# First batch's local attention heads: 32-row query blocks with VectorE's transpositions, or 64-row blocks with TensorE's

## The chip, the cores and the metric

The kernel runs on one core of a Trainium2 chip. Its time is that of the whole program on the device, in microseconds. Three runs of the kernel before took 515.04, 516.04 and 516.3 us, with a median of 516.04 us. TensorE (PE) multiplies matrices, VectorE (DVE) and ScalarE (ACT) do element-wise work, GpSimd (POOL) and SyncE (SP) issue DMA transfers.

## The reference, cut to what matters

Three parts follow each other for a batch of 4, 576 tokens and 8 heads of 64: sparse attention, a channel-mixing block, and four small attention experts. Only the first part is touched. Its first four heads are "local": a query sees itself and the 31 keys before it.

```python
scores = scale * np.matmul(q, k.transpose(0, 1, 3, 2))
mask_local = (rel >= 0) & (rel < stride)                      # stride 32
mask_strided = (rel >= 0) & (pos[None, :] % stride == pos[:, None] % stride)
masks = np.stack([mask_local if h < H // 2 else mask_strided for h in range(H)], axis=0)
scores = np.where(masks[None, :, :, :], scores, -1000000000.0)
scores = scores - np.max(scores, axis=-1, keepdims=True)
attn = np.exp(scores)
attn = attn / (np.sum(attn, axis=-1, keepdims=True) + 1e-09)
x = np.matmul(attn, v)                                        # then the heads side by side
xk = mu_k * x + (1.0 - mu_k) * x_prev ; xr = mu_r * x + (1.0 - mu_r) * x_prev
v = np.maximum(xk @ w_k, 0.0) ** 2 @ w_v ; r = sigmoid(xr @ w_r) ; x = r * v
# x goes on to four gated attention experts, 576 causal tokens each
```

## The kernel before, in words

Nothing is issued where it is written. A recorder (class `Recorder`, lines 185 to 484) collects each operation; `unit` (line 240) names groups of them, and the string `PLAN` (line 21) lists the names in an order of preference. `order` (line 382) is a list scheduler: with costs of its own for each operation it gives each engine's queue, always the operation that it expects to start first, and within 0.1 us of that the one whose unit stands first in `PLAN`. A load into a tile that is still in use isn't given before the scheduler has placed the tile's last user. Where the scheduler expects TensorE to wait within its first 80 us, `warm` (line 371) puts products on a tile of zeros ahead of the waiting operation; they write the result tile that this operation then overwrites, and so bear its name in the trace (`sl<-zeros`). Every engine runs its queue in order.

A name in `PLAN` begins with the batch (0 to 3). `L` with a pair of heads loads its queries, keys and values; of batch 0 it is split into `q`, `v` and `m`, and a plain `0L0` to `0L19` there loads a piece of a weight, `0W` makes it a whole float32, and `0P` splits it into a high and a low part. `S` is scores and softmax, `T` the transposition, `V` the product with the values. `A` and `Z` with r, k, g, m, v are the mixing block's two token chunks (rows 0 to 319 and 320 to 575): preparing its inputs, gates, the first and the second product. Names without a batch's stage letter after `mc` belong to the experts.

Heads go in pairs. Pairs 0 and 1 are local, 2 and 3 strided (`strided_group`, line 844). A local pair is done by `local_part` (line 785) in two parts, `S0` and `S1` for pair 0, `S3` and `S4` for pair 1. The 128 partitions of a score tile hold 2 heads x 2 halves of the sequence (rows 0 to 287 and 288 to 575) x a block of 32 queries, and its columns 5 or 4 such blocks with 64 keys each. `softmax_exp` (line 661) does for each block a masked maximum on VectorE (`CUSTOM_DVE_ANT_0`, tile `el`) and an exponential on ScalarE; `softmax_norm` (line 681) divides on VectorE. VectorE then transposes the 32x32 blocks (`STREAM_TRANSPOSE`, tile `aTl`), and 40 small value products per pair (`pol`) add up in PSUM over both parts, with one unit `V1` or `V4` for the pair. `evac` (line 553) copies a result from PSUM on ScalarE or VectorE, as the scheduler picks.

Loads are in `load`, `load_rest` and `load_more` (lines 710 to 783). Of batch 0's local pairs `near` brings queries and keys in four transfers for blocks 0 to 4 of both halves and four for the rest; `keys` brings the values in eight, which GpSimd issues for batch 0 and SP for the others. The local mask arrives as `mraw`, and six copies on VectorE make the 32-row mask `mloc` of it. Batch 0's local pairs and later those of batch 1 use the two buffers of tile `qkv`.

The first token chunk's gates of batch 0 (`pr<-xw`, units `0Ag0` to `0Ag2`) are the first long products on TensorE; the first of them needs heads 0 to 3 of batch 0 and two pieces of the weight `w_r`.

Of the kernel before, what the change touches and what calls it, by code (L numbers as in the profile page):

```python
# [27 lines left out]
0P8 1Ar0 2L3 0Zm4 2S0 1V8 1Ak0 2S1 1T9 1Ar1 1Ar2 0Zm5 1Ak2 1Zr0 1V9 1Ak1 0Zm6 1Ar3 1Ak3 0Zm7 2S4 2S3 1Zr2 1Zk0 0Zv6  # L28
0Zv2 0P2 0Av7 0P3 0Zv7 1Am0 1Zr3 0Zv4 0Zv0 1Zr1 2V1 1Zk2 2V4 2S7 2Ar0 1Zk1 2S6 1Ag1 3z 1Am1 1Ag3 1Ag0 2T7 1Ag2 0Zv3
1Am2 1Am3 0Zv5 2Zr0 1Am4 2T6 1Zg2 1Am5 2S8 0Zv1 1Zk3 3L1 2V6 2S9 1Zg1 1Am6 2V7 3L0 1Zg0 2T8 1Zg3 2Ar2 1Av0 1Am7 1Av4  # L30
2T9 1Av6 1Zm0 1Zm1 1Zm2 2V9 2V8 1Av2 2Ak0 1Zm3 2Ar3 1Zm4 1Zm5 1Av5 1Zv0 1Av3 1Zm6 1Zm7 1Zv1 1Zv6 2Ak3 1Zv2 2Ar1 2Ak1
2Ak2 1Av1 2Zr2 1Zv4 1Zv7 3L2 3S4 1Av7 2Am0 2Zk0 2Zr3 2Am1 3L3 2Am2 2Ag1 2Ag0 2Ag3 2Am3 1Zv5 2Zr1 3S1 3S0 2Ag2 3S3
3S7 2Av0 3S6 2Am4 3S9 1Zv3 3V1 2Am5 2Am6 2Zg1 2Zk3 2Am7 3S8 3V4 2Zg2 2Zk2 2Zg0 3T7 2Av4 2Zk1 3T6 2Zg3 3V7 2Zm0 2Av6
2Av7 3V6 3T8 2Zm1 2Zm2 3T9 2Zm3 2Av5 3V9 2Av2 2Av3 2Av1 2Zm4 2Zm5 2Zm6 2Zv2 2Zm7 2Zv0 3V8 2Zv6 2Zv4 3Ar0 2Zv1 2Zv7
2Zv3 2Zv5 3Ar1 3Ar2 3Ar3 3Ak0 3Ak1 3Ak2 3Ak3 3Ag0 3Ag1 3Ag2 3Ag3 3Zr0 3Zr1 3Zr2 3Zr3 3Am0 3Am1 3Am2 3Am3 3Am4 3Am5
3Am6 3Am7 3Zk0 3Zk1 3Zk2 3Zk3 3Zg0 3Zg1 3Zg2 3Zg3 wl0 ws00 3Av0 3Av1 3Av2 ws01 3Av3 3Av4 3Av5 wl1 ws10 3Av6 3Av7
ws11 3Zm0 3Zm1 3Zm2 wl2 ws20 3Zm3 3Zm4 3Zm5 3Zm6 ws21 3Zm7 3Zv0 3Zv1 wl3 ws30 3Zv2 3Zv3 3Zv4 ws31 3Zv5 3Zv6 3Zv7 mc
0u 0x0 0k00 0q00 0k01 0q01 0v0 0v1 0x1 0k10 0q10 0k11 0q11 0t 0v2 0v3 0v4 0g 1u 1n 1x0 1k00 0s20 0s21 0s22 1q00 0s23
0s30 1k01 0s31 0s32 1q01 0s33 0m2 0p20 0p21 1v0 0p22 0p23 0s40 1v1 0s41 1x1 1k10 0s10 0m3 1q10 1k11 0s11 0p31 0p33
1q11 0s00 1s20 0m4 0p32 0s13 0s02 0s03 0s01 0p41 0p40 0p30 2x0 2k00 1s23 0s12 2x1 1v2 1s21 1v3 1s30 0m0 1s00 1g 2q01  # L40
0a10 0a11 1s33 1s31 0m1 2k10 1t 2q10 0p11 1s22 0p00 1s03 1s32 2s30 0p13 0o13 0p10 1s01 1m3 0p03 0o11 1m2 2v4 0p01
# [1517 lines left out]
```

## Time and profile before

| | before |
|---|---|
| median of 3 runs | 516.04 us (515.04 to 516.3) |
| profiled execution, its own time | 518.32 us |
| span of that execution | 516.5 us |
| busy: PE, DVE, ACT, POOL | 508.1, 366.5, 301.5, 46.6 us |
| share of the span | 98%, 71%, 58%, 9% |
| chain that ended last | PE 92%, DMA 3%, DVE 3%, ACT 1%, issue 1% |
| granted TensorE clock, mean | 0.997 |

Busy time is an average over stages with different limits: the share of an engine says little until it is read stage by stage. All instructions come from the recorder's line 482, so rows are told apart by their tiles: `sl`, `el`, `aTl`, `pol` are local scores, probabilities, transposed probabilities and results; `ss`, `es`, `pts`, `aTs`, `pos` the same for strided heads; `pr` gates; `xT` the attention's output. A float32 matmul is two MATMUL instructions, a transposition one.

### The profile page before, as it was taken

Reading aid. Unit: us, or ns where it says so; the run is one execution under the profiler, and the core shown is the slowest. Engines: PE = TensorE matmul, PEld = TensorE weight load, DVE = VectorE, ACT = ScalarE, POOL = GpSimd, SP = SyncE. Lnnn points to the kernel's source line nnn. Section 1 sums busy time; section 2 is a strip of 40 time slices with the busy share of each in tenths; the row PEclk is TensorE's granted clock in tenths of the full one; section 3 lists DMA queues with packets and bytes.
Section 4 is the critical chain, followed back from the end, with each engine's and each line's share of the span. In section 5 each row is a group of like instructions: output and inputs, shape, how many; then the busy total and the mean of one; then the engine's idle time right before and its main releaser. Section 6 shows DMA issues by size and latency. Waiting matters only on the chain.

```text
span 516.5 us, 12855 instructions
## 1 busy us (share of the span) xinstructions
PE 508.1 (98%) x4938; PEld 478.1 (93%) x4938; DVE 366.5 (71%) x1320; ACT 301.5 (58%) x893; POOL 46.6 (9%) x104
## 2 busy tenths in 40 slices
...
GB/s 227 330 222 413 129 26 46 136 73 184 10 84 14 90 34 22 11 83 89 67 31 94 82 77 27 31 145 127 70 98 72 51 64 102 32 81 47 13 103 93
...
## 3 DMA queue, kind: packets, MB, share of 16 engines
...
q8 instruction: 39, 0.64, 0.6%
q14 instruction: 22, 0.18, 0.1%
...
## 4 chain that ended last, share of the span: by engine, by line
PE 92%; DMA 3%; DVE 3%; ACT 1%; issue 1%; SPq 0%; ACTq 0%; DVEq 0%
PE pv L482 20%; PE pk L482 20%; PE pr L482 11%; PE pq_True L482 5%; PE pvv L482 5%; PE s L482 5%; PE pq_False L482 5%; PE pt L482 4%; PE pw L482 4%; PE py L482 3%; PE sl L482 3%; PE ss L482 3%; PE pol L482 3%; PE pos L482 2%; PE pts L482 1%; DVE pe L482 1%
## 5 line engine op out<-in xcount | busy, mean ns | idle before, releaser
L482 PE MATMUL pv<-kk,wvh 128*128 128x320 f32 (+1 forms) x512 | 102.8, 295 | 0.0
L482 PEld LDWEIGHTS pv<-kk,wvh 128*128 128x128 f32 x512 | 81.6, 188 | 0.5 <-DVE nm L482 0.2
L482 PE MATMUL pk<-xh,wkh 128*128 128x256 f32 (+1 forms) x224 | 66.6, 297 | 0.0
L482 PE MATMUL pk<-xl,wkh 128*128 128x256 f32 (+1 forms) x224 | 65.3, 291 | 0.0
L482 ACT ACTIVATE rf<-pk 128x320 f32<-128x320 f32 (+1 forms) x64 | 26.1, 407 | 48.9 <-PE pk L482 47.7
L482 ACT ACTIVATE pe<-pe,nm 128x128 f32<-128x128 f32 (+4 forms) x72 | 41.9, 582 | 15.9 <-DVE nm L482 8.0
L482 DVE CAST kk<-rf 128x256 fp32r<-128x256 f32 (+1 forms) x43 | 13.2, 307 | 43.1 <-ACT rf L482 26.9
L482 PEld LDWEIGHTS pk<-xh,wkh 128*128 128x128 f32 x224 | 42.0, 188 | 0.6 <-ACT rf L482 0.2
L482 PEld LDWEIGHTS pk<-xl,wkh 128*128 128x128 f32 x224 | 42.0, 188 | 0.0
L482 DVE CUSTOM_DVE_ANT_0 pe<-s,mcau 128x384 f32<-128x384 f32 (+4 forms) x72 | 33.5, 481 | 5.0 <-PE s L482 4.0
L482 ACT ACTIVATE es<-es,nm 108x108 f32<-108x108 f32 (+1 forms) x80 | 30.2, 381 | 6.6 <-DVE nm L482 6.6
L482 DVE TENSOR_TENSOR sg<-pv,sg 128x320 f32<-128x320 f32 (+1 forms) x32 | 14.5, 452 | 26.0 <-PE pv L482 19.8
L482 PE MATMUL pt<-ident,pe 128*128 128x128 f32 x200 | 30.6, 274 | 0.1
L482 DVE TENSOR_TENSOR kk<-rf,kk 128x320 fp32r<-128x320 f32 (+1 forms) x64 | 28.7, 455 | 2.4 <-ACT kk L482 1.2
L482 ACT ACTIVATE el<-el,nm 128x64 f32<-128x64 f32 x72 | 24.2, 337 | 9.0 <-DVE nm L482 8.8
L482 ACT ACTIVATE rf<-rf 128x320 f32<-128x320 f32 (+1 forms) x64 | 28.4, 444 | 1.3
L482 PE MATMUL pr<-xh,wrh 128*128 128x320 f32 (+1 forms) x96 | 28.7, 299 | 0.0
L482 PE MATMUL pr<-xl,wrh 128*128 128x320 f32 (+1 forms) x96 | 28.2, 294 | 0.0
L482 DVE TENSOR_SCALAR pe<-pe,sm 128x384 f32<-128x384 f32 (+4 forms) x72 | 25.7, 399 | 0.3
L482 DVE SCALAR_TENSOR_TENSOR xf<-xd,mu,xT 128x256 f32<-128x256 f32 (+1 forms) x52 | 25.7, 509 | 0.3
L482 ACT COPY aT<-pt 128x512 f32<-128x512 f32 (+3 forms) x51 | 22.3, 459 | 5.5 <-PE pt L482 5.1
L482 PEld LDWEIGHTS pt<-ident,pe 128*128 128x128 f32 x200 | 23.5, 140 | 1.3 <-issue 0.7
...
## 6 DMA issues: line engine op xcount, KB each, us to landing
...
```

Of the source, the lines that this page charges most:

```text
L482: f[o.engine](*[now(x) for x in a], **{n: now(x) for n, x in k.items()})
```

## The change

Batch 0's local pairs are done in three thirds of 192 rows instead of two interleaved parts, by a new function `local_third`: 128 partitions hold 2 heads x a block of 64 queries, the columns 3 blocks with 96 keys each. Each third has units of its own for `S`, `T` and `V` (`0S0` to `0S5`, `0T0` to `0T5`, `0V0` to `0V5`). TensorE transposes the 128x96 blocks against the identity, into PSUM, and `evac` copies them out; each third's result is copied out by itself. The loads of batch 0's local pairs are cut by thirds: pair 0 in four transfers for its first two thirds, pair 1 in two, with the values in 64-row blocks of 96 keys, all on SP; the last third comes in `m`. The mask is used as it arrives; the six copies that make the 32-row mask stand in batch 1's load of pair 0. Batches 1 to 3 compute as before. `PLAN` is another order up to the experts (`mc`); behind that its names follow in the same order.

```diff
--- before.py
+++ after.py
@@ -19,34 +19,35 @@
 P = 128
 BIG = 3.0e38
 PLAN = """
-0z 0L0 0L0q 0L0m 0L1q 0L2q 0S0 0L1m 0S1 0L2v 0L1v 0L1 0i 0L0v 0L3q 0S3 0S4 0V1 1L1 0V4 0S6 0L3v 1L0 0W0 0L2 0S7 0L3
-0Ar0 0T6 0L4 0L5 0L6 2z 0T7 0Ar1 1z 0V6 0W1 0V7 0L7 0L8 0S9 0L9 0T9 1L2 0W2 0S8 0Zr0 0W3 0W6 0V9 0T8 0L10 0Ar2 0L11
-0V8 0L12 0L13 0W4 0W7 0Ar3 0Ag0 1S0 0Ak0 0W5 0L14 0W10 0Ak1 0L15 1S1 0L16 0W9 0Ak3 0Zr1 0Zr3 0W12 0Zk0 0W13 1L3 0Zr2
-0L17 0Ak2 0P12 0Zg3 0W14 0Zg0 0W11 0Ag1 0Am0 0W8 0Zg2 0Am1 0W15 0Am2 0W17 0Am3 0P13 0W16 1S4 0Am4 0L18 0Am5 0P6 0P14
-0W18 0P17 0P15 0Am6 0L19 0P18 0Ag2 0Am7 0W19 0P19 0Age 1S3 1V1 0P9 0Zg1 0Av4 0Av6 0P16 2L0 1S6 0Av0 0Av2 1S7 1V4 0P4
-2L1 1S8 0Zk3 0sig 0Av5 0P5 0Av3 1T7 1T6 0P10 0Zk2 0Av1 0Zk1 0P7 0Zm0 0Zm1 1S9 1V6 0P11 1V7 0P0 0Zm2 2L2 0P1 0Zm3 1T8
...
+0L1q 0z 0L0q 0i 0L2q 0L1v 0S3 0L0 0S4 0T3 0V3 0L3q 0L3v 0L1 0L0v 0L0m 0L2v 0S1 0L1m 0W1 0W0 0T4 0S0 0L2 0S6 0T1 0L3
+1L1 0L4 0L5 0V4 0S7 0L6 0L7 0T0 0V0 0V1 0Ar0 0T6 0V6 0Ar1 0T7 0S9 1L0 0L8 0T9 0Ak0 1z 0L9 0W2 0L10 0Ak1 0S8 1L2 0W6
+0T8 0V7 0W3 0S2 0Ar2 0V9 0S5 0T5 0L11 0T2 0V8 0L12 0Ag0 0Ak2 0Ar3 0Ak3 0W7 0W4 0V2 0W5 0Am0 0L13 1S1 0L14 0L15 1S3
+0W9 1S0 0L16 0L17 0Zr0 0Am1 0W12 0W11 0W8 1S4 0W13 0Zr2 0W10 0V5 0P13 0Am2 1L3 2z 0Zk0 0Am3 1V1 0W14 0Am4 0Am5 0P12
+0L18 0Zr3 0L19 0P14 0W16 0W15 0P15 0Am6 0P16 0W17 0Zr1 3z 0P5 0P6 0Am7 0W18 0Ag1 0Zg0 0Zg3 0Zg2 0W19 0Av6 0P18 0Ag2
+1V4 0Zg1 0Age 0P19 0Av0 0P4 0Av4 0P17 1S7 2L0 0sig 1S6 1T7 0Zk3 2L1 0Av7 0Zk1 0Av2 0P10 2L2 0P8 0Av5 0Zk2 2L3 1T6
...
 """
 WHOLE = {(1, 0)}
 POC = (1, 2)
@@ -574,8 +575,8 @@
 
     nc.zeros = p1.tile([P, P], F32, tag="zeros", name="zeros", bufs=1)
     nc.zeros.at = 2.7
-    mraw = p1.tile([P, 2, LK], F32, tag="mraw", name="mraw", bufs=1)
-    mloc = p1.tile([P, 2, 64], F32, tag="mloc", name="mloc", bufs=1)
+    mloc = p1.tile([P, 2, LK], F32, tag="mloc", name="mloc", bufs=1)
+    mblk = p1.tile([P, 2, 64], F32, tag="mblk", name="mblk", bufs=1)
     mstr = {}
     for nr in (7, 6):
         n = NN * nr
@@ -717,60 +718,56 @@
                 else:
                     t = p1.tile([P, LW], F32, tag="qkv", name=f"qkv{b}_{hp}")
                 kw = S + 32 if local else S
-                c = S + kw
-                w = src.shape[1]
-
-                def part(a, z):
-                    nc.sync.dma_start(t[:, a:z], src[:, a:z])
-
-                def keys():
-
+                if b == 0:
+
+                    c = S + kw
+                    w = src.shape[1]
+
+                    def part(a, z):
+                        nc.sync.dma_start(t[:, a:z], src[:, a:z])
+
+                    n = 3 * LQ
+                    if hp == 0:
+                        part(0, n)
+                        part(S, S + n + 32)
+                        nc.sync.dma_start(mloc, c_loc)
+                        part(n, 2 * n)
+                        part(S + n + 32, S + 2 * n + 32)
+                    elif local:
+                        part(0, 2 * n)
+                        part(S, S + 2 * n + 32)
+                    else:
+                        part(0, c)
+                    z = c + 6 * 2 * D if local else w
+                    st["rest"] = lambda: part(c, z)
+                    st["more"] = [(2 * n, S), (S + 2 * n + 32, c), (z, w)]
+                    st["part"] = part
+                elif local:
+                    c = S + kw
+                    nc.sync.dma_start(t[:, :c], src[:, :c])
                     x = src[:, c:].rearrange("p (i h d) -> p i h d", h=2, d=D)
-                    v = t[:, c:c + 10 * D].rearrange("p (m d) -> p m d", d=D)
+                    st["blocks"] = t[:, c:c + 10 * D].rearrange("p (m d) -> p m d", d=D)
                     for u, m, r, i in ((0, 0, 0, 0), (0, 1, 32, 0), (1, 0, 32, 4), (1, 1, 64, 4)):
                         for h in range(2):
                             q = 64 * h + 32 * u
-                            (nc.sync if b else nc.gpsimd).dma_start(v[q:q + 32, m::2, :], x[r:r + 32, i:i + 5, h, :])
-                    st["v"] = v
-
-                if local:
-                    T0, H = 5 * 32, S // 2
-                    st["keys"] = keys
-
-                    def near(a, z):
-                        for o in (0, H):
-                            part(o + a, o + z)
-                            part(S + o + a + 32 * (a > 0), S + o + (H if z == H and o == 0 else z + 32))
-
-                    st["more"] = lambda: near(T0, H)
-                if b == 0:
-                    if local:
-                        near(0, T0)
-                        if hp == 0:
-                            nc.sync.dma_start(mraw, c_loc)
-                            for q in range(4):
-                                qs = slice(32 * q, 32 * q + 32)
-                                if q % 2 == 0:
-                                    nc.vector.tensor_copy(mloc[qs, :, :], mraw[qs, :, :64])
-                                else:
-                                    for i in range(2):
-                                        nc.vector.tensor_copy(mloc[qs, i, :], mraw[qs, 1, 32:])
-                    else:
-                        part(0, c)
-                        st["rest"] = lambda: part(c, w)
-                elif local:
-                    part(0, c)
-                    keys()
+                            nc.sync.dma_start(st["blocks"][q:q + 32, m::2, :], x[r:r + 32, i:i + 5, h, :])
+                    if b == 1 and hp == 0:
+                        for q in range(4):
+                            qs = slice(32 * q, 32 * q + 32)
+                            if q % 2 == 0:
+                                nc.vector.tensor_copy(mblk[qs, :, :], mloc[qs, :, :64])
+                            else:
+                                for i in range(2):
+                                    nc.vector.tensor_copy(mblk[qs, i, :], mloc[qs, 1, 32:])
                 else:
-                    part(0, w)
+                    nc.sync.dma_start(t[:, :src.shape[1]], src)
                 st["q"] = t[:, :S]
                 st["k"] = t[:, S:S + kw]
-                if not local:
-                    st["v"] = t[:, c:w].rearrange("p (i h d) -> p i h d", h=2, d=D)
+                st["v"] = t[:, S + kw:src.shape[1]].rearrange("p (i h d) -> p i h d", h=2, d=D)
 
             def load_rest():
                 if b == 0:
-                    st["keys" if local else "rest"]()
+                    st["rest"]()
                     if hp == 1:
                         for i, nr in enumerate((7, 6)):
                             nc.sync.dma_start(mstr[nr], c_str[i, :NN * nr, :NN * nr])
@@ -778,9 +775,65 @@
 
             def load_more():
                 if b == 0:
-                    st["more"]()
+                    for a, z in st["more"]:
+                        st["part"](a, z)
 
             loads.append((load, load_rest) + (load_more,) * (b == 0 and local))
+
+            def local_third(hf):
+
+                def sc_f():
+                    sc = score(f"sl{b}_{hp}_{hf}", (hp, hf) in LCM)
+                    for g in range(3):
+                        i = 3 * hf + g
+                        for h in range(2):
+                            hs = slice(D * h, D * h + D)
+                            nc.tensor.matmul(
+                                sc[hs, g * LK:(g + 1) * LK],
+                                st["q"][hs, LQ * i:LQ * i + LQ],
+                                st["k"][hs, LQ * i:LQ * i + LK],
+                                start=True, stop=True,
+                            )
+                    st["sc", hf] = sc
+
+                def ex_f():
+                    e = p1.tile([P, 2, 324], F32, tag="e", bufs=3, name=f"el{b}_{hp}_{hf}")
+                    e = e.rearrange("p a b -> p (a b)")[:, :3 * LK].unsqueeze(1)
+                    st["sm", hf] = softmax_exp(
+                        [st["sc", hf]], e, P, 3, LK,
+                        lambda g: mloc[:, 0 if hf == 0 and g == 0 else 1, :],
+                        f"{b}_{hp}_{hf}",
+                    )
+                    st["e", hf] = e
+
+                def no_f(part=None):
+                    softmax_norm(st["sm", hf], st["e", hf], P, 1, 3, LK, f"{b}_{hp}_{hf}", part)
+
+                def tr_f():
+                    e = st["e", hf]
+                    aT = p1.tile([P, 2, 324], F32, tag="aT", name=f"aTl{b}_{hp}_{hf}")
+                    aT = aT.rearrange("p a b -> p (a b)")
+                    pt = ps_tr(f"ptl{b}_{hp}_{hf}")
+                    for g in range(3):
+                        nc.tensor.transpose(pt[:LK, g * P:(g + 1) * P], e[:, 0, g * LK:(g + 1) * LK], ident)
+                    evac(aT[:LK, :3 * P], pt[:LK, :3 * P])
+                    st["aT", hf] = aT
+
+                def av_f():
+                    aT = st["aT", hf]
+                    po = values(f"pol{b}_{hp}_{hf}")
+                    for g in range(3):
+                        for h in range(2):
+                            nc.tensor.matmul(
+                                po[D * h:D * h + D, g * LQ:(g + 1) * LQ],
+                                st["v"][:LK, 3 * hf + g, h, :],
+                                aT[:LK, g * P + h * LQ:g * P + (h + 1) * LQ],
+                                start=True, stop=True,
+                            )
+                    n = 3 * LQ
+                    evac(xTs[b][:, hp, 1 + n * hf:1 + n * hf + n], po[:, :n])
+
+                return sc_f, ex_f, no_f, tr_f, av_f
 
             def local_part(hf):
 
@@ -807,7 +860,7 @@
                     e = e.rearrange("p a b -> p (a b)")[:, :n * 64].unsqueeze(1)
                     st["sm", hf] = softmax_exp(
                         [st["sc", hf]], e, P, n, 64,
-                        lambda g: mloc[:, 0 if hf == 0 and g == 0 else 1, :],
+                        lambda g: mblk[:, 0 if hf == 0 and g == 0 else 1, :],
                         f"{b}_{hp}_{hf}",
                     )
                     st["e", hf] = e
@@ -832,7 +885,7 @@
                                 x = 32 * max(0, 2 * m - 1)
                                 nc.tensor.matmul(
                                     po[u][D * h:D * h + D, 32 * a:32 * z],
-                                    st["v"][q:q + 32, m, :], aT[q:q + 32, x:x + 32 * (z - a)],
+                                    st["blocks"][q:q + 32, m, :], aT[q:q + 32, x:x + 32 * (z - a)],
                                     start=(m == 0), stop=(m == 9),
                                 )
                     n = S // 2
@@ -896,7 +949,12 @@
 
                 return sc_f, ex_f, no_f, tr_f, av_f
 
-            stages.extend([local_part(i) for i in range(2)] + [None] if local else [strided_group(i) for i in range(2)])
+            if not local:
+                stages.extend(strided_group(i) for i in range(2))
+            elif b == 0:
+                stages.extend(local_third(i) for i in range(3))
+            else:
+                stages.extend([local_part(0), local_part(1), None])
 
         stages, loads = [], []
         for hp in range(NHP):
@@ -913,7 +971,7 @@
             else:
                 nc.unit(f"{b}L{hp}", lambda l=l: several(*l))
         for i, f in enumerate(stages):
-            if i >= 6:
+            if b == 0 or i >= 6:
                 nc.unit(f"{b}S{i}", lambda f=f: several(*f[:3]))
                 nc.unit(f"{b}T{i}", f[3])
                 nc.unit(f"{b}V{i}", f[4])
```

## Rows read from the trace of the kernel before

**Rows 1.** stretches: us, busy PE, PEld, DVE, ACT, POOL; clock, DMA, GB/s

```profile
8.80:20.00 11.20, 11.20 (x198) 10.11 (x201) 6.64 (x56) 6.65 (x36) 1.88 (x4) 1.00 1.05 287
20.00:30.00 10.00, 8.87 (x162) 7.86 (x154) 5.95 (x31) 6.67 (x29) 0.00 (x0) 0.83 0.83 263
30.00:39.00 9.00, 8.90 (x68) 6.93 (x69) 9.00 (x37) 7.49 (x29) 0.37 (x1) 1.00 0.88 283
39.00:52.00 13.00, 13.00 (x126) 10.10 (x123) 12.97 (x50) 9.78 (x33) 0.00 (x0) 1.00 1.03 413
91.00:104.00 13.00, 11.71 (x164) 11.00 (x165) 11.30 (x47) 10.24 (x40) 0.00 (x0) 1.00 0.44 132
195.00:325.00 130.00, 130.00 (x1254) 128.24 (x1247) 77.94 (x258) 66.07 (x182) 0.20 (x1) 1.00 0.18 57
```

**Rows 2.** readers of zeros: ns shortest/median/longest, first and last start

```profile
L482 PE MATMUL sl<-zeros x42: 421/421/476, 1.1 to 15.8; 128*128 128x64 f32 x42
```

**Rows 3.** timeline to 33 us: start, us, engine, instruction [idle before]

```profile
3.07 0.43 SPq L482 DMA_DIRECT2D mraw<-in_c_loc_dram  x1
...
7.61 1.16 DVE L482 COPY mloc<-mraw 32x128 f32<-32x128 f32 x6 [0.86 <-DMA mraw<-in_c_loc_dram]
...
8.82 0.22 DVE L482 CUSTOM_DVE_ANT_0 el<-sl,mloc 128x64 f32<-128x64 f32 x1
...
25.02 0.92 PE L482 MATMUL pol<-aTl,qkv 32*64 32x64 f32 x27 [1.13 <-issue]
...
32.59 0.81 PE L482 MATMUL pr<-xw,w('r', 0)_98 128*128 128x320 f32 x2
```

**Rows 4.** who waited for whom, 8.8 to 33 us: total, times, longest

```profile
DVE el L482 <- PE sl L482: 4.1, 3, 1.7
```

**Rows 5.** groups by shape, 0 to 40 us: count | busy us, mean ns | idle before

```profile
L482 ACT ACTIVATE el<-el,nm 128x64 f32<-128x64 f32 x18 | 6.1, 338 | 6.8 <-DVE nm L482 6.8
...
L482 ACT ACTIVATE es<-es,nm 108x108 f32<-108x108 f32 x12 | 4.5, 379 | 0.0
...
L482 DVE CUSTOM_DVE_ANT_0 el<-sl,mloc 128x64 f32<-128x64 f32 x18 | 3.1, 216 | 4.2 <-PE sl L482 4.1
...
L482 DVE CUSTOM_DVE_ANT_0 es<-ss,mstr 108x108 f32<-108x108 f32 x12 | 2.8, 258 | 1.9 <-PE ss L482 1.9
...
L482 ACT COPY aTs<-pts 108x324 f32<-108x324 f32 x4 | 1.5, 431 | 0.4 <-PE pts L482 0.4
...
L482 ACT COPY xT<-pol 128x288 f32<-128x288 f32 x4 | 1.4, 403 | 3.1 <-PE pol L482 3.1
...
L482 DVE STREAM_TRANSPOSE aTl<-el 128x320 f32<-128x320 f32 x2 | 1.0, 506 | 0.0
...
L482 DVE TENSOR_TENSOR el<-el,sm 128x320 f32<-128x320 f32 x2 | 1.0, 488 | 0.0
...
L482 DVE RECIPROCAL sm<-sm 128x5 f32<-128x5 f32 x2 | 0.4, 187 | 0.0
```

**Rows 6.** chain of waits, 0 to 130 us: start, us, what (matmul instructions)

```profile
36.09 0.56 PE pts L482 x6
...
38.17 1.22 PE pos L482 x20
...
43.36 1.14 PE sl L482 x72
...
60.16 1.30 PE pol L482 x80
...
79.87 0.75 PE ss L482 x12
```

**Rows 7.** timeline of SP, 18 to 35 us

```profile
20.71 12.56 SPq L482 DMA_DIRECT2D qkv<-in_loc_dram  x18
33.31 1.86 SPq L482 DMA_DIRECT2D wraw<-in_w_k_dram  x4
```

**Rows 8.** timeline of TensorE at its one hole

```profile
95.86 0.71 PE L482 MATMUL ss<-qkv 64*126 64x126 f32 x8 [1.29 <-DMA qkv<-in_strd_dram]
```

More of the change, by code (lines that the diff above doesn't have):

```diff
@@ L27 @@
-2L1 1S8 0Zk3 0sig 0Av5 0P5 0Av3 1T7 1T6 0P10 0Zk2 0Av1 0Zk1 0P7 0Zm0 0Zm1 1S9 1V6 0P11 1V7 0P0 0Zm2 2L2 0P1 0Zm3 1T8
[L28 to L41, printed above, removed]
@@ L47 @@
-2p03 3m2 3s40 3s00 2p41 2p10 3q01 3s41 1o02 2a10 2a11 3s03 2a00 2a01 3m4 3s01 3m3 3p23 3s02 3p21 3p30 3p41 1o03 3p33
-3p20 3s12 3p40 3m0 3p22 2o12 3s11 2o02 2o11 3p32 3p31 3p01 3s13 3m1 3p00 2o10 3p11 2o00 2o13 3p13 3p03 3p02 2o03
-2o01 3p10 3a10 3p12 3a11 3a00 3a01 3o11 3o13 3o03 3o00 3o12 3o10 3o01 3o02
+0L1q 0z 0L0q 0i 0L2q 0L1v 0S3 0L0 0S4 0T3 0V3 0L3q 0L3v 0L1 0L0v 0L0m 0L2v 0S1 0L1m 0W1 0W0 0T4 0S0 0L2 0S6 0T1 0L3
+1L1 0L4 0L5 0V4 0S7 0L6 0L7 0T0 0V0 0V1 0Ar0 0T6 0V6 0Ar1 0T7 0S9 1L0 0L8 0T9 0Ak0 1z 0L9 0W2 0L10 0Ak1 0S8 1L2 0W6
@@ new lines @@
+0T8 0V7 0W3 0S2 0Ar2 0V9 0S5 0T5 0L11 0T2 0V8 0L12 0Ag0 0Ak2 0Ar3 0Ak3 0W7 0W4 0V2 0W5 0Am0 0L13 1S1 0L14 0L15 1S3
+0W9 1S0 0L16 0L17 0Zr0 0Am1 0W12 0W11 0W8 1S4 0W13 0Zr2 0W10 0V5 0P13 0Am2 1L3 2z 0Zk0 0Am3 1V1 0W14 0Am4 0Am5 0P12
+0L18 0Zr3 0L19 0P14 0W16 0W15 0P15 0Am6 0P16 0W17 0Zr1 3z 0P5 0P6 0Am7 0W18 0Ag1 0Zg0 0Zg3 0Zg2 0W19 0Av6 0P18 0Ag2
+1V4 0Zg1 0Age 0P19 0Av0 0P4 0Av4 0P17 1S7 2L0 0sig 1S6 1T7 0Zk3 2L1 0Av7 0Zk1 0Av2 0P10 2L2 0P8 0Av5 0Zk2 2L3 1T6
+0P7 0Zm0 0Zm1 0Zm2 0Av1 1Ar0 0Zm3 1S8 3L0 1V6 0P3 1V7 1S9 1Ar2 0P2 1Ak0 0P9 0Av3 1Ak2 0P11 0Zm4 1T8 1Ar1 0Zm5 1T9
@@ new lines @@
+0P1 1Zr0 1V9 2S1 1V8 0Zm6 1Ar3 0Zm7 0Zv2 1Ak3 0Zv0 2S0 0Zv3 0Zv4 2S4 0Zv1 2V1 2S3 1Ak1 1Am0 1Zr2 0Zv6 1Am1 0P0 1Am2
+0Zv7 1Ag2 1Am3 1Am4 2S7 0Zv5 1Am5 1Ag3 1Zr1 1Zr3 1Zk0 1Ag1 1Ag0 1Am6 1Zg0 2Ar0 2S6 1Zk1 1Zg1 2S8 1Av6 1Zk3 2V4 1Zk2
+2T7 1Am7 1Zg2 3L1 2T6 2V6 1Zg3 1Zm0 2Ar1 2Ak0 1Av4 1Av2 1Av3 1Zm1 2V7 1Zm2 1Zm3 1Av0 2Zr0 1Zv6 1Zm4 2S9 2T8 2T9 1Zm5
+2V8 2Ar2 1Zm6 1Zm7 2V9 2Ar3 1Zv2 1Av5 1Av7 2Ag1 2Ak3 2Ak2 3S1 1Zv3 2Ag2 2Zk0 3L2 2Ak1 3S0 1Zv7 1Zv4 2Zr1 2Zr2 1Av1
+2Ag3 2Zr3 2Ag0 2Zk2 1Zv5 2Am0 2Am1 2Zk3 3S3 3S4 3S6 1Zv0 2Zg1 3V1 2Zg2 2Am2 2Am3 2Am4 2Av2 1Zv1 2Zg0 2Am5 2Am6 2Av0
@@ new lines @@
+3V4 2Am7 3T6 2Zk1 2Zg3 2Av4 2Zm0 2Zm1 2Av6 2Av7 2Zm2 3L3 3S7 2Zm3 2Zm4 2Zm5 3T7 3S8 2Av5 3S9 3V6 3T8 2Av3 2Av1 3T9
+3V7 2Zm6 3V8 3V9 2Zm7 2Zv0 2Zv1 2Zv2 2Zv3 2Zv4 2Zv5 2Zv6 2Zv7 3Ar0 3Ar1 3Ar2 3Ar3 3Ak0 3Ak1 3Ak2 3Ak3 3Ag0 3Ag1 3Ag2
+3Ag3 3Zr0 3Zr1 3Zr2 3Zr3 3Am0 3Am1 3Am2 3Am3 3Am4 3Am5 3Am6 3Am7 3Zk0 3Zk1 3Zk2 3Zk3 3Zg0 3Zg1 3Zg2 3Zg3 wl0 ws00
+3Av0 3Av1 3Av2 ws01 3Av3 3Av4 3Av5 wl1 ws10 3Av6 3Av7 ws11 3Zm0 3Zm1 3Zm2 wl2 ws20 3Zm3 3Zm4 3Zm5 3Zm6 ws21 3Zm7
+3Zv0 3Zv1 wl3 ws30 3Zv2 3Zv3 3Zv4 ws31 3Zv5 3Zv6 3Zv7 mc 0u 0x0 0k00 0q00 0k01 0q01 0v0 0v1 0x1 0k10 0q10 0k11 0q11
@@ new lines @@
+0t 0v2 0v3 0v4 0g 1u 1n 1x0 1k00 0s20 0s21 0s22 1q00 0s23 0s30 1k01 0s31 0s32 1q01 0s33 0m2 0p20 0p21 1v0 0p22 0p23
+0s40 1v1 0s41 1x1 1k10 0s10 0m3 1q10 1k11 0s11 0p31 0p33 1q11 0s00 1s20 0m4 0p32 0s13 0s02 0s03 0s01 0p41 0p40 0p30
+2x0 2k00 1s23 0s12 2x1 1v2 1s21 1v3 1s30 0m0 1s00 1g 2q01 0a10 0a11 1s33 1s31 0m1 2k10 1t 2q10 0p11 1s22 0p00 1s03
+1s32 2s30 0p13 0o13 0p10 1s01 1m3 0p03 0o11 1m2 2v4 0p01 0p02 2q00 2q11 1s02 1p31 2k11 2u 2k01 0p12 1s40 0a00 1s41
+1m0 0a01 1s10 2v3 1p20 1s12 2t 1m4 2v2 1p32 0o12 3x1 2v0 1s11 1s13 1p30 3x0 0o02 1p40 1p41 2v1 2s20 2s33 1p33 1m1
```

12 lines of the change are left out of this document (7 added, 5 removed).

## The prediction

> **What bounds the kernel now.** I read the table of busy time by stretch first, then the instructions that read the tile of zeros, the timeline of the first 33 us, the list of who waited for whom, the groups of instructions by shape, and the chain of waits. In the table, TensorE is busy for all of 195 to 325 us and of 39 to 52 us, with VectorE at 60% in the first of these stretches and at 99.8% in the second [rows 1]. So the long middle is TensorE's, and nothing of the change lies there. The end of the kernel can move only by how early TensorE's unbroken work begins, by holes in it, and by work put into it.
>
> It begins at 32.59 us with the first gate product `pr` [rows 3]. Before that TensorE only looks busy: 42 products on the tile of zeros stand between 1.1 and 15.8 us under the name of the first local scores [rows 2], and later there is a bare stall of 1.13 us on issue at 25.02 [rows 3]. What is late in that stretch is the first batch's softmax. Its first masked maximum stands only at 8.82 us, after six copies that build the 32-row mask and that waited for the mask's transfer until 7.61 [rows 3]. From 8.8 to 30 us VectorE is idle for 11.20 - 6.64 + 10.00 - 5.95 = 8.6 us and ScalarE for 11.20 - 6.65 + 10.00 - 6.67 = 7.9 us [rows 1]; VectorE's largest wait there is 4.1 us, for local scores [rows 4]. From 30 to 52 us VectorE has no idle time, while ScalarE has 1.5 + 3.2 us [rows 1]: a supply that just keeps up.
>
> **The change part by part.** Sums are made against the profiled execution, 518.32 us (span 516.5 and 1.8 us around it); the runs shown have a median of 516.04, 2.28 us less, and I move the difference over to that median.
>
> *Earlier first softmax.* The mask's transfer was SP's sixth, issued at 3.07 us and waited for until 7.61: 4.5 us [rows 3]. After, it is SP's fifth, behind two larger transfers of the second pair and two of the first; at SP's 0.43 us per issue [rows 3] that is about 2.6 us, so it lands near 7.1 at the latest, and no copies of 1.16 us stand ahead of the first use. The first softmax begins near 6.8 us: 2.0 us gained, of which 0 to 3 are possible, as the larger transfers need more or less time than four small ones. The copies come back at the second batch's load, on VectorE, inside the full stretch; their 1.2 us are 0.6 on each engine if others move over, and I set that off against the evictions, which can all go to ScalarE's slack.
>
> *Work of the local heads on VectorE and ScalarE* (all from [rows 5], both pairs). Before: 18 maxima of 0.216 and 18 exponentials of 0.338 make 10.0 us; 4 normalisations of 288 columns on average, 0.45 by the 320-column row, with two small instructions of 0.187 each make 3.3; 4 transpositions of about 0.455 make 1.8; 4 evictions of 0.403 make 1.6; together 16.7. After: 18 of each over 96 columns instead of 64; between the 64-column and the 108-column rows these are about 0.247 and 0.368, so 11.1; 6 normalisations 4.9; no transposition on VectorE; but 6 evictions of transposed tiles (384 columns; the rows at 288 and 324 columns lead to 0.48) 2.9, and 6 result evictions of 192 columns, about 0.32, 1.9. Together 20.8, or 3.47 a third: 4.1 us more for the two engines.
>
> At this point the Trainium skill speaks against the change. The page "VectorE: DVE Perf Modes", section "Rules for kernel authors", calls VectorE's own transposition the fastest for blocks of 32, and the section "The three transpose paths" adds that TensorE's lands in PSUM, so that it needs an eviction. By that rule this edit costs time wherever either engine is full, and the second rival would be the case. The rows [rows 5] show per 288 columns 0.455 against an eviction of 0.48: nearly level, but the first can only be VectorE's time and the second may be ScalarE's.
>
> *Less of it ahead of TensorE.* Before, both halves of each pair interleave rows 0 to 287 and 288 to 575, so all 16.7 us stand ahead of the first token chunk (rows 0 to 319). After, thirds 0 and 1 of each pair suffice: 4 x 3.47 = 13.9 us. That is 2.8 us less, 1.4 us on each of two engines.
>
> *Fewer waits.* Before, SP issues sixteen transfers of queries and keys for the two pairs and GpSimd sixteen of values. After, six on SP bring everything that four thirds of scores need, and the values come in two transfers per pair. The waits of 8.6 and 7.9 us before 30 us are for scores whose data came in pieces, for `pol` behind the issue stall, and for zeros queued ahead. They can go wholly (8 us) or not at all, since `0L0v`, the first pair's values, now stands behind about 4 MB of other loads (by the tiles' shapes), and its `V` units must wait for it. I take 3 us, under the middle, as an engine's waits here are mostly for another engine. The gate products so begin 2.0 + 1.4 + 3 = 6.4 us earlier, near 26 us.
>
> *What is owed later.* The third thirds (`0S2`, `0S5` with their `T` and `V`) now fall into the full stretch: 6.9 us over two engines, 3.45 us each. On TensorE, before: 72 local-score matmuls take 1.14 us and 80 value matmuls 1.30 per pair [rows 6], two matmuls to a product; 4.9 in all, wholly ahead of 32.59. After, a third has 6 score products of 96 columns; from 0.75 for 6 of 108 columns [rows 6], 0.67; 3 transpositions at 0.56/6, 0.28; 6 value products of 64 columns; from 1.22 for 10 of 115 on average [rows 6], 0.41; so 1.36. Unknown is how far the two heads' products overlap in this form: as well as the 32-row ones (1.14/36 and 1.30/40 per product, the scores scaled by columns) a third takes 0.76; as the strided rows unscaled, 1.76. I take the middle, scaled from the rows nearest in shape. Two thirds in the dense part cost 2.7 us (1.5 to 3.5). TensorE does that while the other engines do theirs, so the larger debt counts, not the sum: 3.45 us. The other four thirds lie in TensorE's idle front.
>
> *SP.* Before, the second batch's local loads hold SP for 12.56 us from 20.71, and most loads of `w_k` are issued only from 33.31 [rows 7]. After, those local loads can't start before a pair's last third has given its tile back, so weights go first: no weight is later than now. What is later is the second batch, whose scores fill gaps there. I cost it at nothing; its price without cover is the third rival.
>
> *Order up to the dense part.* The only hole that the timeline shows on TensorE from 33 to 104 us is 1.29 us ahead of `ss` at 95.86, a wait for a strided load [rows 8]. It may stay or go: 0, bounds -1.3 and +1.3. Later instructions are the same in number and kind.
>
> Sum: -6.4 + 3.45 = -2.95, say -3.0 us: 515.3 for the profiled execution, 513.0 for the median.
>
> **The rivals.**
> *The waits go wholly.* If everything needed is on chip from 7 us and both engines run through, 8 us come back instead of 3: -7.95, 508.1. For it: the transfers are larger, and fewer issues pace them. Against: the late values of the first pair, and engines that wait for each other.
> *The lead is eaten.* From 30 to 52 us VectorE has nothing spare [rows 1]. If the third thirds' 6.9 us fall on VectorE alone, because what ScalarE takes over pushes other work back, the debt doubles: -6.4 + 6.9, 516.5. For it: VectorE at 100%. Against: ScalarE's 4.7 us, and 13.00 - 11.30 + 13.00 - 10.24 = 4.5 us idle on both at 91 to 104 us [rows 1]. The skill's rule on transpositions would lead here.
> *The second batch comes too late (slower).* Its local loads wait for tiles that the third thirds hold. Before they were issued from 20.71 on [rows 7]; if the last local `V` unit comes after about 45 us, its softmax (some 17 us over two engines, as the first's) is pushed to where only the 4.5 us above are idle. Then 17 - 4.5 = 12.5 us, 6.2 on each engine, come too late for the second batch's gates, and the kernel takes 516.04 - 2.95 + 6.2 = 519.3. For it: in-order SP, where a load that waits for a tile holds all behind it, as the 12.56 us show. Against: weights still to be split keep the engines fed meanwhile.
> That the change does not do what it says is no case: the units of the plan show the thirds.
>
> **How the numbers follow.** Forecast 513.0, its own range 510 to 514.4: chance 0.49. Waits go wholly (below 510): 0.15. Lead eaten (514.4 to 517.6): 0.19. Slower: 0.17. A measurement of this kernel can tell about 0.3%, 1.55 us, from no change, so faster is 0.49 + 0.15 = 0.64, same 0.19, slower 0.17. The range of 8 in 10 runs from 507.5, the first rival with half of the hole of 1.3 gone as well, to 517.6, which leaves out most of the slower case.
>
> **What would show it.** First local maximum before 7.5 us; first `pr` at 24 to 28 us; less than half as many products on zeros; no transposition on VectorE before 40 us; `0S2` and `0S5` behind the first `pr`; most `w_k` loads issued before 30 us; no hole over 1.5 us on TensorE from 33 to 104 us. It is wrong if `pr` begins after 30 us, or if it begins early and holes of more than 3 us open behind it.

## The result, and the profile after

The changed kernel takes 511.21 us (median of 8 runs, 510.34 to 513.49), the kernel before beside it 516.35 us: ratio 0.9896, 95% interval 0.9862 to 0.993. Run again among the experiments it took 512.26 us (12 runs, 510.26 to 516.36) against 516.1: 0.9925, interval 0.9899 to 0.995. By these ratios it is faster by 3.9 to 5.4 us, where 3.0 was forecast. The profiled execution shown here took 511.24 us, its span is 509.5.

The table of busy time by stretch, after (columns as in [rows 1]):

```profile
8.80:20.00 11.20, 10.77 (x116) 8.70 (x114) 9.23 (x65) 9.09 (x42) 0.00 (x0) 1.00 0.99 348
20.00:30.00 10.00, 9.03 (x93) 6.42 (x91) 10.00 (x40) 8.70 (x35) 0.10 (x1) 1.00 1.01 398
30.00:39.00 9.00, 9.00 (x65) 5.92 (x64) 9.00 (x25) 9.00 (x27) 0.00 (x0) 1.00 1.02 411
39.00:52.00 13.00, 13.00 (x50) 9.20 (x49) 12.32 (x31) 12.77 (x28) 0.00 (x0) 1.00 0.84 263
91.00:104.00 13.00, 13.00 (x186) 12.49 (x187) 12.28 (x63) 11.66 (x52) 0.00 (x0) 1.00 0.45 119
195.00:325.00 130.00, 130.00 (x1102) 128.64 (x1101) 71.20 (x213) 63.91 (x157) 0.00 (x0) 1.00 0.16 51
```

From 8.8 to 30 us VectorE is now idle for 11.20 - 9.23 + 10.00 - 10.00 = 2.0 us (before 8.6), ScalarE for 2.1 + 1.3 = 3.4 us (before 7.9). From 39 to 52 us ScalarE is busy for 12.77 us instead of 9.78: the slack of [rows 1] is used up. The hole at 91 to 104 us [rows 8] is gone.

The timeline after, all engines (start, us, engine, instruction, idle before), for [rows 3] and [rows 7]:

```profile
2.58 0.43 SPq L483 DMA_DIRECT2D mloc<-in_c_loc_dram  x1
...
5.83 0.26 DVE L483 CUSTOM_DVE_ANT_0 el<-sl,mloc 128x96 f32<-128x96 f32 x1 [4.83 <-DMA mloc<-in_c_loc_dram]
...
6.90 0.51 DVE L483 COPY mblk<-mloc 32x128 f32<-32x128 f32 x3
...
18.93 4.95 SPq L483 DMA_DIRECT2D wraw<-in_w_k_dram  x8
...
37.21 14.81 SPq L483 DMA_DIRECT2D qkv<-in_loc_dram  x18
```

The first masked maximum stands at 5.83 us (8.82 before). The six copies for the second batch's mask did come back, but on VectorE from 6.90 us on, not inside the full stretch. The weights `w_k` are all issued by 23.9 us, and the second batch's local loads begin at 37.21.

TensorE's timeline after:

```profile
13.12 0.57 PE L483 MATMUL pol<-aTl,qkv 96*64 96x64 f32 x12
...
14.58 0.82 PE L483 MATMUL ss<-qkv 64*108 64x108 f32 x12
...
19.81 0.71 PE L483 MATMUL sl<-qkv 64*64 64x96 f32 x12
...
21.77 0.71 PE L483 MATMUL sl<-qkv 64*64 64x96 f32 x12
22.41 0.77 PE L483 MATMUL pts<-ident,es 108*108 108x108 f32 x6
...
23.51 0.81 PE L483 MATMUL pr<-xw,w('r', 0)_335 128*128 128x320 f32 x2
...
27.13 0.81 PE L483 MATMUL pr<-xw,w('r', 0)_335 128*128 128x320 f32 x2 [0.52 <-DVE nm L483]
...
38.97 0.70 PE L483 MATMUL pk<-xw,w('k', 0, 0)_569 128*128 128x320 f32 x2
```

The first gate product `pr` is at 23.51 us (32.59 before), unbroken from 27.13 on. The scores of the third thirds stand at 19.81 and 21.77, ahead of it. The last row, the first product `pk` of the mixing block, is the mark by which the runs below are read: from it to the end of the span are 509.5 - 38.97 = 470.5 us.

**The same kernel in another execution.** The profiled run of the repetition took 516.36 us (span 514.6), 5.1 more than the one above. Its TensorE timeline:

```profile
13.34 0.91 PE L483 MATMUL pol<-aTl,qkv 96*64 96x64 f32 x12
...
15.83 1.42 PE L483 MATMUL ss<-qkv 64*108 64x108 f32 x12
...
28.03 1.21 PE L483 MATMUL pts<-ident,es 108*108 108x108 f32 x6
...
29.26 0.76 PE L483 MATMUL pr<-xw,w('r', 0)_335 128*128 128x320 f32 x2
...
31.19 0.77 PE L483 MATMUL pts<-ident,es 108*108 108x108 f32 x6
...
44.09 0.70 PE L483 MATMUL pk<-xw,w('k', 0, 0)_569 128*128 128x320 f32 x2
```

The queues are the same, and at 13 us the two executions are 0.22 us apart. But twelve score instructions `ss` take 1.42 us instead of 0.82 and six transpositions 1.21 instead of 0.77. By these lengths (the last section sets them beside a granted clock) TensorE ran at its lower level (1.2 GHz) beyond 28.03 us here, and only until about 13 us in the first execution. At `pk` the lag is 5.12 us, and from `pk` to the end are 514.6 - 44.09 = 470.5 us, as above. What happens in the front reaches the end one for one. Its stretches:

```profile
8.80:20.00 11.20, 11.20 (x87) 9.13 (x85) 7.66 (x52) 7.88 (x35) 0.00 (x0) 1.00 1.01 354
20.00:30.00 10.00, 10.00 (x85) 8.29 (x85) 7.48 (x29) 5.76 (x23) 0.00 (x0) 1.00 1.03 416
```

Here TensorE is the full engine of the front, and VectorE idles for 3.5 + 2.5 = 6.1 us, ScalarE for 7.6. A single profile of this front is therefore good for 5 us either way, and sizes are read from medians and ratios. It also bears on the gain: with TensorE at its lower level through the front, the changed kernel took 516.36 us, no less than the median of the kernel before (516.1). Of the twelve executions of the repetition two took that long (516.08 and 516.36; only the second has a trace), the other ten 510.3 to 513.4 us.

### The profile page after: what moved, and what is told of

It is laid out like the page before. It is cut to its first block, busy times and chain, and to the rows that moved or that the text cites. A ratio compares the mean times of both kernels' runs of the same rounds, so it can differ in the third digit from the quotient of the medians.

```text
span 509.5 us, 12492 instructions
## 1 busy us (share of the span) xinstructions
PE 502.7 (99%) x4766; PEld 471.2 (92%) x4766; DVE 363.1 (71%) x1318; ACT 306.0 (60%) x905; POOL 36.9 (7%) x88
## 4 chain that ended last, share of the span: by engine, by line
PE 96%; ACT 2%; DVE 1%; DMA 1%; issue 0%; SPq 0%; ACTq 0%
PE pk L483 21%; PE pv L483 20%; PE pr L483 11%; PE s L483 6%; PE pvv L483 5%; PE pw L483 5%; PE pq_True L483 5%; PE pq_False L483 5%; PE pt L483 4%; PE py L483 4%; PE sl L483 2%; PE ss L483 2%; PE pol L483 2%; PE pos L483 2%; PE pts L483 1%; ACT es L483 1%
## 5 line engine op out<-in xcount | busy, mean ns | idle before, releaser
L483 DVE CAST kk<-rf 128x320 fp32r<-128x320 f32 (+1 forms) x45 | 13.9, 310 | 39.7 <-ACT rf L483 35.0
L483 ACT ACTIVATE el<-el,nm 128x64 f32<-128x64 f32 (+1 forms) x72 | 24.7, 345 | 6.6 <-DVE nm L483 6.5
L483 ACT COPY sg<-pr 128x320 f32<-128x320 f32 (+1 forms) x31 | 12.2, 401 | 23.4 <-PE pr L483 23.2
```

The source lines that it names most:

```text
L483: f[o.engine](*[now(x) for x in a], **{n: now(x) for n, x in k.items()})
```

## The experiments

By the medians no run but the one that leaves work out was faster than the changed kernel.

**The control.** No edit.

> The changed kernel once more, beside which the others of this call are read. Both theories: 511.2 us, ratio to the kernel before 0.990, from the eight runs of the result.

Measured 512.26 us, 0.9925: as above.

**VectorE's work doubled in place, in both kernels.**

```diff
-                f[o.engine](*[now(x) for x in a], ...)
+                again = o.token in TWICE and "accum_out" in k and "in1" in k
+                for _ in range(1 + again):
+                    f[o.engine](*[now(x) for x in a], ...)
```

> The changed kernel with the 18 masked maxima of the first batch's local heads issued twice, in place, everything else in the same order on the same engines: 18 x 0.18 us at their pitch in the trace, 3.2 us more on VectorE, 2.2 of them ahead of 30 us. The second maximum reads the same scores, so the output stays what it was. Theory of the supply (VectorE now runs with under 2 us idle from 8.8 to 30 us, so what it does there sets the gates): 1.5 to 3 us slower than the changed kernel, the gates as much later. Rival (front supply is immaterial, the gain came from the weights loaded earlier and from the hole near 95 us that is gone): no difference, within 0.5 us.

> The kernel before with the 18 masked maxima of the first batch's local heads issued twice, in place, as was done to the changed kernel, where it cost 3.0 us. 18 x 0.145 us at their pitch, 2.6 us more on VectorE. Theory (in the kernel before transfers and their order set the pace of the front, and VectorE waits 8.6 us from 8.8 to 30 us): the waits take it up, 0 to 1 us slower. Rival (VectorE's own work sets the gates in both kernels): 2.6 us slower, 518.5 us or more.

Measured: on the changed kernel 515.29 us, 0.9984 (0.9954 to 1.0013), 3.0 us more than the control; on the kernel before 515.89 us, 0.9974 (0.9939 to 1.0009), nothing. The stretches of the doubled kernel before:

```profile
8.80:20.00 11.20, 11.20 (x198) 10.12 (x201) 10.05 (x90) 7.56 (x36) 2.00 (x4) 1.00 0.93 255
20.00:30.00 10.00, 8.90 (x182) 7.85 (x177) 8.88 (x43) 8.57 (x35) 0.00 (x0) 1.00 0.90 290
```

VectorE's idle time fell from 8.6 to 1.15 + 1.12 = 2.3 us and the end did not move: before, the waits were real room. (Part of that fall is this execution's own, whose first `pr` stands at 30.38 us, 2.2 us ahead of the profile before.) After, the median rose by 3.0 us, nearly all of the 18 x 0.18 = 3.2 us added: there VectorE's work is on the path. It is not alone on it. In the chain of waits of the first profile after, ScalarE leads from 13.23 to 22.11 us, mostly with the strided exponentials, and VectorE after it:

```profile
15.98 1.66 ACT es L483 x9
...
22.11 0.88 DVE xd L483 x2
```

And the profiled execution of the doubled changed kernel, the slowest of its twelve (518.44 us), had TensorE at its lower level until about 28 us and VectorE idle for 1.7 + 2.7 = 4.4 us:

```profile
8.80:20.00 11.20, 10.90 (x84) 8.73 (x80) 9.46 (x66) 8.02 (x35) 0.00 (x0) 1.00 1.02 364
20.00:30.00 10.00, 10.00 (x88) 8.02 (x86) 7.31 (x29) 6.39 (x27) 0.00 (x0) 1.00 1.01 368
```

So the theory of the supply rests on the times of both kernels; which engine leads differs between executions.

**The first transfers cut small.**

```diff
+                n = {"0L0q": 2, "0L1q": 4}.get(o.token, 1)
...
+                w = dst.cols.size
+                for i in range(n):
+                    p, q = w * i // n, w * (i + 1) // n
+                    f[o.engine](now(dst)[:, p:q], src[:, p:q])
```

> The changed kernel with the six first transfers of queries and keys of the two local pairs cut into sixteen, so that SP issues as many as in the kernel before; nothing else is changed. Theory (fewer, larger transfers are what took the waits out of the front): at SP's 0.43 us for each of ten more issues, with eight in flight at most, the first softmax and all loads behind come 2 to 4 us later, the time rises by 1.5 to 4 us and VectorE's idle time from 8.8 to 30 us goes back over 5 us. Rival (the transfers were not it; the place of the identity, the mask and the strided pair in the order is): the time rises by less than 1 us.

Measured 516.03 us, 0.9994 (0.9956 to 1.0031): 0.69% or 3.6 us over the control, the whole gain gone. Its timeline of SP:

```profile
0.74 5.60 SPq L493 DMA_DIRECT2D qkv<-in_loc_dram  x12
6.38 0.43 SPq L488 DMA_DIRECT2D mloc<-in_c_loc_dram  x1
```

VectorE's timeline of the same run, where the first maximum waits for that transfer:

```profile
8.68 0.26 DVE L488 CUSTOM_DVE_ANT_0 el<-sl,mloc 128x96 f32<-128x96 f32 x1 [7.68 <-DMA mloc<-in_c_loc_dram]
```

And its stretches:

```profile
8.80:20.00 11.20, 9.04 (x73) 7.22 (x75) 6.88 (x51) 7.12 (x32) 0.00 (x0) 1.00 0.94 315
20.00:30.00 10.00, 9.93 (x113) 8.29 (x114) 8.67 (x43) 8.67 (x38) 0.00 (x0) 1.00 0.97 345
```

Ten more issues put the mask's transfer at 6.38 instead of 2.58 us and the first maximum at 8.68, where it stood before the change; VectorE idles for 4.3 + 1.3 = 5.7 us. So the number of first transfers is shown to be a cause, worth as much as the whole gain. By which way is not shown: the edit delays the first softmax, all later loads (the identity is issued at 8.76 instead of 4.00 us), and in this execution TensorE, whose first scores now wait for data, left its lower level only at about 23.6 us instead of 13. What the first softmax is worth by itself was not measured.

**The third thirds left out.**

```diff
+LATE = {f"0{u}{i}" for u in "STV" for i in (2, 5)}
...
+                if o.token in LATE:
+                    if a and a[0].tile.shape[1:] == [4, 577]:
+                        self.nc.gpsimd.memset(now(a[0]), 0.0)
+                    continue
```

> The changed kernel without the third thirds of the first batch's two local pairs: scores, softmax, transpositions and result products of rows 384 to 575 are left out, and those rows of xT are set to zero by GpSimd; the rest keeps its order. The prediction charged these thirds 3.45 us (6.9 us of VectorE and ScalarE work over two engines that are full) and, on TensorE, at least 2 x 1.36 beside it. Theory of the debt: 3 to 3.5 us less than the changed kernel, 508 to 509 us. Rival (the thirds run in gaps, as 0S2 and 0S5 stand at 19.8 and 21.8 us, ahead of the first gate product): within 1 us of the changed kernel.

Measured 509.9 us, 0.9849 (0.9798 to 0.9901): 2.4 us under the control by the medians, 3.9 by the ratios. In its TensorE timeline `pk` comes 2.7 us earlier than in the first profile after:

```profile
36.26 0.70 PE L488 MATMUL pk<-xw,w('k', 0, 0)_521 128*128 128x320 f32 x2
```

The rival (within 1 us) is unlikely, as four of the six runs lie under the lowest of the control (510.26); the charge of 3.45 us lies inside what was measured. The size is not better known than that: the interval touches the control's (0.9899 to 0.995), and in the profiled execution TensorE left its lower level at about 9 us instead of 13 and had a granted clock of 0.57 and 0.58 again from 22 to 26 us, so its 2.7 us are not those of the thirds alone.

**Blocks and order apart.** `PLAN` rewritten: the old order with `0S0 0T0`, `0S1 0T1 0S2 0T2`, `0V0 0V1 0V2` for pair 0 (alike for pair 1), or the new order without the tokens that only the thirds have.

```diff
-0L1q 0z 0L0q 0i 0L2q 0L1v 0S3 0L0 0S4 0T3 0V3 0L3q ...
+0z 0L0 0L0q 0L0m 0L1q 0L2q 0S0 0L1m 0S1 0L2v 0L1v 0L1 0i 0T0 0T1 0S2 0T2 ...
```

> The 64-row blocks in the order of the kernel before: the two halves of each of the first batch's local pairs are replaced by its three thirds, all ahead of the chunk, and the rest of the order is the old one. Theory of the blocks (the 64-row form, with its fewer and larger transfers, is what takes the waits out of the front): the first gate product still comes before 29 us, VectorE's idle time from 8.8 to 30 us is under 4 us, and the time is 512 to 514 us; what is missing to 511.2 are the 3.5 us of third thirds that again stand ahead of TensorE's work. Rival, the order (it is the new sequence, with the strided pair first and the weights earlier, that keeps the engines fed): VectorE is idle for over 7 us as before, the gates begin after 31 us, and the time is 515.5 to 519 us.

> The 32-row blocks in the new order: where the new order names a pair's thirds, the two halves stand. Theory of the blocks: sixteen small transfers of values, sixteen of queries and keys and the six copies of the mask stay, so the gates begin after 31 us and the time is 515 to 518 us. Rival, the order: gates before 28 us, the hole near 95 us gone, 511 to 513 us.

Measured 528.53 us, 1.0226 (1.0193 to 1.026), and 529.6 us, 1.025 (1.0223 to 1.0277). Both theories missed: each half of the change alone, in the one form of it that was tried, makes the kernel 2.3 to 2.5% slower. TensorE's timelines show long runs of zeros in front of real work, with the new blocks in the old order

```profile
16.41 5.38 PE L482 MATMUL ptl<-zeros 128*128 128x64 f32 x24
```

and with the old blocks in the new order

```profile
6.06 10.50 PE L482 MATMUL sl<-zeros 128*128 128x64 f32 x48
```

**The zeros taken out**, to see if they were the reason: only the first group stays.

```diff
+        self.warmed = False
...
+        if self.warmed:
+            return
+        self.warmed = True
```

> The changed kernel with the first group of products on zeros alone (8 instructions at 1.05 us); the later groups, 20 instructions, are left out, all else in the same order. Theory of the queue (a group of zeros that stands ahead of a transposition or a score is a delay: VectorE waited 0.61 us for ptl at 10.96 and 1.00 us at 13.23 behind them): 510.5 to 511.7 us, 0.5 to 1 us less. Rival, the clock (the zeros keep TensorE at it and so bring the full rate, at which a product on zeros goes from 213 to 112 ns, earlier): the full rate comes later, 513 to 516 us.

> The kernel before with the first group of products on zeros alone (20 instructions from 1.05 us); 38 later ones are left out. Theory of the queue: the 22 instructions at 213 ns ahead of local scores between 8.40 and 16.1 us, 4.7 us, were a good part of VectorE's waits, so 512.5 to 514.5 us: the change won much of its 5 us by having fewer of them. Rival, the clock: 516.5 to 520 us. Third theory (transfers set the pace of the front, so a gap is a gap with zeros in it or without): 515.5 to 516.5 us.

> The 64-row blocks in the old order, as in the run that took 528.5 us, with the first group of products on zeros alone (16 instructions). In that run 24 of them, 5.4 us, stood ahead of the first transposition at 21.6 us, while VectorE was idle. If those were what cost it 12 us against the kernel before: 514 to 518 us. If the old order does not fit the new blocks by itself (transfers of the strided pair behind those of the local ones, third thirds ahead of the chunk): 524 us or more.

> The 32-row blocks in the new order, as in the run that took 529.6 us, with the first group of products on zeros alone (10 instructions). In that run 48 of them, 10.5 us, stood ahead of the second pair's scores from 6.06 on, and 22, 4.95 us, ahead of the first result products. If those were what cost it 13 us: 514 to 518 us. If the small transfers and the mask's copies did: 524 us or more.

Measured: new blocks and order 512.7 us, 0.9898 (0.9856 to 0.994); old ones 517.21, 1.0003 (0.9971 to 1.0036); new blocks in the old order 530.89, 1.0239 (1.0184 to 1.0294); old blocks in the new order 528.73, 1.0214 (1.017 to 1.0259). None differs from its twin with zeros beyond the interval: the zeros stood in gaps that were there anyway, and of the theories on them only the third one (a gap is a gap, with zeros in it or without) holds. With them gone TensorE's timelines name its longest waits in the first 30 us, with the new blocks in the old order

```profile
17.44 2.28 PE L486 MATMUL ptl<-ident,el 128*96 128x128 f32 x9 [3.24 <-DMA ident<-in_c_ident_dram]
```

and with the old blocks in the new order

```profile
15.50 0.42 PE L486 MATMUL sl<-qkv 64*32 64x64 f32 x2 [9.50 <-DMA qkv<-in_loc_dram]
```

The new blocks need the identity matrix for their first transposition, and the old order loads it late. The old blocks' next scores waited 9.5 us for queries and keys that come in small pieces, which the new order puts behind other loads.

**Two places of the order moved** in the first of the two: the identity `0i`, with the transpositions `0T0` and `0T1` now directly behind their scores, and the third thirds, with `0Zr0` behind them.

```diff
-0z 0L0 0L0q 0L0m 0L1q ... 0S0 0L1m 0S1 ... 0L1 0i 0T0 0T1 0S2 0T2 ... 0S4 0T4 0S5 0T5 0V0 0V1 0V2 ... 0S8 0Zr0 0W3 ... 0L11 0V8 0L12 ...
+0z 0L0 0L0q 0i 0L0m 0L1q ... 0S0 0T0 0L1m 0S1 0T1 ... 0L1 ... 0S4 0T4 0V0 0V1 ... 0S8 0W3 ... 0L11 0V8 0S2 0S5 0T5 0T2 0V2 0V5 0Zr0 0L12 ...
```

> The 64-row blocks in the old order, as in the run that took 528.5 us, but with two places changed: the identity matrix is loaded fourth instead of twenty-second (in that run's form without zeros TensorE's first transposition waited 3.2 us for it, until 17.4 us), and the third thirds stand behind the gate units of the chunk instead of ahead of it. Theory (these two places are what the new blocks need; the rest of the search is worth little): 511 to 515 us. Rival (the whole sequence matters: strided pair first, the weights behind it, second batch's loads behind all weights): 519 us or more.

Measured 523.58 us, 1.0104 (1.0056 to 1.0152). Between the two theories, nearer to the rival: the two places give back 1.2 to 1.35%, 6 to 7 us, of some 17 to the changed kernel. What is left, by its TensorE timeline:

```profile
42.35 2.42 PE L482 MATMUL pr<-xw,w('r', 3)_458 128*128 128x320 f32 x8 [2.05 <-DVE xw L482]
...
50.25 0.70 PE L482 MATMUL pk<-xw,w('k', 0, 0)_547 128*128 128x320 f32 x2
```

The last gates wait for VectorE, 3.68 us of zeros stand behind them at 44.61 us, and `pk` begins at 50.25 us although `pr` did at 25.51. Which further places are at fault was not tried.

## Why the prediction was right, and what in it was not

*The bound.* Right. From `pk` on the span lasts 470.5 us in both profiles of the changed kernel and 507.0 - 36.26 = 470.7 without the thirds; what these executions differ by arose in the front. (The mark does not compare the two kernels: in the kernel before `pk` stands behind the second chunk's gates, at 50.25 us, 466.2 ahead of the end.) What the prediction did not see is that TensorE itself can be the slow engine there: its text has the front wait for VectorE and ScalarE alone, and 5.1 us between two executions hang on the level at which TensorE runs. Its own range, 510 to 514.4, is narrower than that. So it is in part luck that the forecast came near: it knew nothing of the level, and its 3 us for the waits were chosen between 0 and 8.

*Earlier first softmax: the term that was mis-sized.* Forecast 6.8 us and 2.0 gained; measured 5.83 and 3.0. I let the mask land "near 7.1 at the latest", 4.5 us after its issue as before. It was waited for until 5.83, 3.25 us after its issue at 2.58. The step stood for 2.0 of the 6.4 us that the gates were to gain; the first maximum came 8.82 - 5.83 = 3.0 us earlier, and if the gates gained as much, about 1 us of the 0.9 to 2.4 us that the forecast lacks lies here. With the first softmax back at 8.68 us in the run with cut transfers the whole gain was gone, but that edit delayed more than the mask.

*Work per third.* Near. The groups by shape, after (count | busy us, mean ns | idle before):

```profile
L483 ACT ACTIVATE el<-el,nm 128x96 f32<-128x96 f32 x18 | 6.5, 365 | 4.4 <-DVE nm L483 4.3
...
L483 DVE CUSTOM_DVE_ANT_0 el<-sl,mloc 128x96 f32<-128x96 f32 x18 | 4.0, 251 | 6.1 <-DMA mloc<-in_c_loc_dram 4.8 <-PE sl L483 0.7 <-PE ptl L483 0.6
...
L483 ACT COPY aTl<-ptl 96x384 f32<-96x384 f32 x5 | 2.3, 472 | 2.1 <-PE ptl L483 2.1
```

The chain of waits, after (start, us, what):

```profile
34.93 0.66 PE ptl L483 x6
...
36.67 0.50 PE pol L483 x12
```

Maximum 0.251 (0.247 forecast), exponential 0.365 (0.368), eviction 0.472 on ScalarE (0.48). On TensorE three transpositions 0.33, six result products 0.50 (0.41), and scores 20.46 - 19.81 = 0.65: 1.48 a third against 1.36.

The rule of the Trainium skill that spoke against the change ("VectorE: DVE Perf Modes", "Rules for kernel authors": VectorE's own transposition is the fastest for blocks of 32) did not decide the time of the whole change, which has other parts; no run changes the transposition alone. The eviction that TensorE's form needs was paid: one of the six ran on VectorE at 15.14 us, five on ScalarE, and 0.35 + 0.36 us of these stand in the chain of waits, at 13.23 and 17.64 us. The rival that followed from the rule, the lead eaten, would have been 516.5 us; 511.2 and 512.3 were measured.

*Fewer waits, 3 us.* VectorE won back 6.6 us and ScalarE 4.5 in the first profile, 2.5 and 0.3 in the second. With 3.0 for the first softmax, the prediction's 1.4 for less work ahead, which no run measures, and 2.4 to 3.9 owed, the measured 3.9 to 5.4 leave 2 to 5 us for the waits; 3 is inside, but this is a remainder and not a measurement. Of the causes named, many small transfers are shown by the run with cut ones; zeros queued ahead were none, as the runs without them show; the issue stall ahead of `pol` was not tested.

*Owed later, 3.45 us.* Inside the 2.4 to 3.9 measured. That `0S2` and `0S5` stand behind the first `pr` was wrong; their transpositions and products do.

*Order, 0 (±1.3).* The one hole I looked at, 1.29 us, went, which is inside the bounds and was not counted as gain. As a view of the order the step was wrong: the old order, as translated here, costs 16 to 18 us with these blocks. The step took order and blocks as two terms that add up. They do not: 1.0226 and 1.025 apart, 0.9925 together.

*The rivals.* The waits did not go wholly (508.1). The second batch did not come too late: the last local result product of the first batch starts at 37.83 us, ahead of 45. Of the signs, the first maximum, the zeros (28 instructions instead of 58), `w_k` before 30 us, no transposition on VectorE before 40 us and no hole on TensorE came as said; the first `pr`, forecast for 24 to 28, stood at 23.51 in one execution and at 29.26 in the other.
